# Collecting the first output tile in two free banks during the last attention head

## The chip, the cores and the metric

The kernel runs on one core of a Trainium2 chip. The metric is the device time of one execution in microseconds (us), read as the median of several runs. A profile of one execution on the chip stands beside the times. Its engines are PE (TensorE matmuls; PEld are its weight loads), DVE (VectorE), ACT (ScalarE), POOL (GpSimd) and SP (SyncE, which here only issues transfers). L363 is line 363 of the kernel.

## The reference, cut to what matters

One transformer block on a sequence of 2048 rows of 640 numbers. `h` is a modulated layer norm of `x`; the attention has 32 heads of 128 with keys and values from a cache of 2048 rows; its output goes through `wo`, is scaled by `ga` and added to `x`. A second, mixer-like part follows.

```python
q = (x @ wq) -> (heads, 2048, 128)
p = softmax(q @ k_cache^T * 128 ** -0.5)
o = p @ v_cache                                  # per head
A = o (2048 x 4096) @ wo                         # 4096 = 32 heads x 128
x = x + ga * A
x = x + gb * B(layernorm(x) * (1 + cb) + sb)     # two layer norms, shifts, four products
```

## The kernel before, in words

**Steps.** The sequence is cut into 16 tiles of 128 rows (`NQT`), so there are 32 x 16 = 512 tiles of attention (`NG`), counted by `g`: head `g // 16`, tile `g % 16`. The main loop (L636) runs over steps `s`. In step `s` PE makes the scores of tile `s` in two halves of 1024 columns (`qk`, L342, with the second matmul of each half at L15), into the two halves of the PSUM tensor `Sps`; DVE scales each half, copies it to `negS` and takes its minimum (L675); POOL joins the two minima (L680); ACT writes the exponentials to a slot of `ring` (L683). The score matrix must be transposed before the product with the values. That happens for groups of up to three tiles by a DMA transpose that SP issues (`transpose`, L282 to L286, shown as L284), or for a few single tiles (`PE_AT`) by PE: `t_piece` (L309, transposes at L316) puts a quarter of the tile into one of two banks, `Oaug` or `QPp` (`JB`), and `t_evac` (L320, L323) copies them back to the ring with ACT. Ten steps after its scores (`PVD = 10`) a tile gets its value product (`pv`, L355, matmuls at L363) in `PTp`; ACT copies two tiles at a time out of it (L660), POOL divides by the sum of the exponentials (L540, L547) and writes four tiles to `o_scratch` in DRAM (L554).

**Ring slots.** A planner written in Python (L235 to L277) gives each tile a slot for its exponentials (`PSL`) and one for its transpose (`TSL`). The ring has six windows of three slots (`WIN`) for groups and two single slots (`ONE`) for PE's tiles. `first_of` and `last_of` say in which step a group's window is taken and in which its transpose is issued. By it, in the last head, tiles 497, 504 and 511 go to PE and 498-500, 501-503, 505-507 and 508-510 go by DMA; tile 504's transposes lie in steps 508 and 509, tile 511's in 514 and 515. The exponentials of 508-510 go to slots 0 to 2, which held those of 501-503 until their transpose was done.

**PE's order.** It is the order of the program. In each half step: scores, value product, then at most one piece more: a fifth of a later head's projection (`q_piece`, L296, in all heads but the last) or two transposes. In the last head the two `JB` banks hold only transposes.

**The product with wo.** `load_ot` (L595, shown as L596) fetches a pair of tiles for some heads out of `o_scratch`, transposed, into `OTj`. `a_pe` (L615) multiplies one tile of it with `wo` for some heads (matmuls at L624): for each head one of 512 and one of 128 columns, into a half of `Sps` (`YB`). Tile 0 is made in three parts, `OTC = [0, 12, 24, 32]` heads: two in steps 517 and 518, the last behind the loop; tile 1 has 12 heads in step 520 and the others behind the loop. From then on each tile follows the one before (`a_two`, `a_pe`), with DVE's scaling, sum and norm (`a_s1`, L730, first instruction L732; `a_s2`). The x tiles for the sum come by `load_xt` (L603, L604).

**SP's order** from step 496 on: group 494-496, load of tile pair 0, heads 0 to 11 (step 498), groups 498-500, 501-503, 505-507, load of heads 12 to 23 (step 507), group 508-510, then at step 513 load of heads 24 to 31, x tiles 0 to 3, pair 1 in two halves, and the other x tiles.

Every operation names what it reads and writes (`r=`, `w=`); `Prog` (L20) turns that into semaphore waits.

Of the kernel before, what the change touches and what calls it, by code (L numbers as in the profile page):

```python
# [123 lines left out]
def bass_adaLN_cond__mha_block_cached__mixer_s_mlp__prompt_kernel(  # L124
# [21 lines left out]
    with ExitStack() as es:  # L146
# [9 lines left out]
        if True:  # L156
            with ExitStack() as es1:
# [2 lines left out]
                PVD = 10  # L160
                PE_T = {3: 7, 10: 14, 17: 21, 24: 28, 31: 37}
                PE_AT = {32 * i + t: 32 * i + a for i in range(NG // 32) for t, a in PE_T.items()}
                PE_AT[NG - 1] = NG + 2
                US = KT * (SQ + 4)
                small = sb1("small", [128, 4 * NQT + 32], F32)
                ring = sb1("ring", [128, NS, SK], BF16)
# [74 lines left out]
                def take(opts):  # L241
                    a = min((a for a in opts if free_at[a] is not None), key=lambda a: free_at[a])
                    free_at[a] = None
                    return a
# [10 lines left out]
                    trios.append(m)  # L255
                    todo = todo[len(m):]
                for m in trios:
                    first_of[m[0]] = last_of[m[-1]] = m
                for s in range(NG):
                    end = s >= NG - 10  # L260
                    g = s - PVD
                    if g in PSL and is_pe(g):
                        free_at[TSL[g]] = 100 + s
                    elif g in last_of:
                        free_at[TSL[last_of[g][0]]] = 100 + s + 1
                    if is_pe(s):
                        PSL[s] = TSL[s] = take(ONE)
                    if s in first_of:
                        a = take(WIN[0:3] if end else WIN)
                        for i, g in enumerate(first_of[s]):  # L270
                            PSL[g] = a + i
                    if s in last_of:
                        m = last_of[s]
                        a = take(WIN[3:6] if end else WIN)
                        for i, g in enumerate(m):
                            TSL[g] = a + i
                        free_at[PSL[m[0]]] = 100 + s + 6.5  # L277
# [25 lines left out]
                def q_evac(h, cc):  # L303
# [2 lines left out]
                    G.op("scalar", lambda a: a.copy(QT[:, hb, cc * 512:(cc + 1) * 512], JB[jb]),  # L306
                         r=[("J", jb)], w=[("QT", hb, cc)])

                def t_piece(g, r, q):  # L309
                    jb = bank(("t", g, r))  # L310
                    src = ring[:, PSL[g], :].bitcast(F32)

                    def f(t):
                        for z in range(2 * q, 2 * q + 2):
                            c0 = (4 * r + z) * 128
                            ins = t.transpose(JB[jb][:, z * 128:(z + 1) * 128], src[:, c0:c0 + 128], identf[:])  # L316
                        return ins
                    G.op("tensor", f, r=[("PT", PSL[g], r), "identf"], w=[("J", jb)])

                def t_evac(g, r):  # L320
                    jb = bank(("t", g, r))
                    dst = ring[:, TSL[g], r * 1024:(r + 1) * 1024].bitcast(F32)
                    G.op("scalar", lambda a: a.copy(dst, JB[jb]), r=[("J", jb)], w=[("PT", TSL[g], r)])  # L323

                PIECES = []
                taken = [u for a in PE_AT.values() for u in range(2 * a, 2 * a + 4)]
# [278 lines left out]
                        xt[:, 4 * c0:4 * c1], x2d[c0 * 512:c1 * 512, :].rearrange("(t p) d -> p t d", p=128)),  # L605
                        ("xt", c0), w=[("x1", t) for t in range(4 * c0, 4 * c1)] + ringk(XT0 + 4 * c0 * D, XT0 + 4 * c1 * D))

                OTC = [0, 12 * H // 32, 24 * H // 32, H]
                yn = [0]

                def ybank():
# [3 lines left out]
                def a_pe(j, b=None, parts=(0, 1, 2), hs=None):  # L615
                    if b is None:
                        b = ybank()
                    pr, z = divmod(j, 2)
                    h0, h1 = hs or (OTC[parts[0]], OTC[parts[-1] + 1])

                    def f(t):
                        for c0, cw in NC2:
                            for hh in range(h0, h1):
                                ins = t.matmul(YB[b][:, c0:c0 + cw], OTj[pr % 2][:, 2 * hh + z, :], wo[:, hh, c0:c0 + cw],  # L624
                                               start=(hh == 0), stop=(hh == H - 1))
                        return ins
                    G.op("tensor", f, r=[("OT", pr % 2, i) for i in parts] + [("OTa", pr % 2)] + ["wo", "woz", "wo4"], w=[("S", b)])
                    return b

                def a_two(j):  # L630
                    b = a_pe(j, None, (0,), (0, H // 2))
                    return a_pe(j, b, (1, 2), (H // 2, H))

                YB = [Sps[:, 0:1024], Sps[:, 1024:2048]]
                LAG = 4
                for s in range(NG + PVD + LAG):  # L636
                    h, j = divmod(s, NQT)
                    g_ = s - PVD
                    evacs = []
                    for half in range(2):  # L640
                        if s < NG:
                            qk(s, half)
                        if half == 0 and s in (NG + PVD - 5, NG + PVD - 4):
                            b0 = a_pe(0, None if s == NG + PVD - 5 else b0, (s - NG - PVD + 5,))
                        if half == 0 and s == NG + PVD - 2:
                            b1 = a_pe(1, None, (0,))
                        if 0 <= g_ < NG:
                            pv(g_, half)
                        if h + 1 < H and 2 * s + half in PIECES[h]:
                            cc, q = PIECES[h][2 * s + half]  # L650
                            q_piece(h + 1, cc, q)
                            if q == KT - 1:
                                evacs.append((q_evac, h + 1, cc))
                        for g, r in t_of(s):
                            t_piece(g, r, half)
                            if half == 1:
                                evacs.append((t_evac, g, r))
                    if 0 <= g_ < NG and g_ % 2 == 1:
                        p = g_ // 2
                        G.op("scalar", lambda a, p=p: a.copy(  # L660
                            Of[:, p % 4].rearrange("p z d -> p (z d)")[:, 0:259], PO[:, (p % 2) * 512:(p % 2) * 512 + 259]),
                            r=[("O", p % 2)], w=[("Of", p % 4)])
# [16 lines left out]
                    if s < NG:  # L679
                        G.op("gpsimd", lambda g, r8=r8: g.tensor_scalar(  # L680
                            out=nm[:, r8:r8 + 1], in0=nm0[:, r8:r8 + 1], scalar1=nm1[:, r8:r8 + 1], scalar2=None, op0=ALU.min),
                            r=[("nmh", 0, r8), ("nmh", 1, r8)], w=[("nm", r8)])
                        G.op("scalar", lambda a, s=s, r8=r8: a.activation(  # L683
                            ring[:, PSL[s], :], negS[:, s % 3, :], ACT.Exp, bias=nm[:, r8:r8 + 1], scale=-1.0),
                            r=[("negS", s % 3), ("nm", r8)], w=slot(PSL[s]))
                        for fn, *args in LATE.get(s, ()):
                            fn(*args)
                        if s in last_of:
                            transpose(last_of[s])
                        if j == 2 and h >= 1 and h + 1 < H:  # L690
                            load_k(h + 1)
                        if h + 1 == H and j in (2, PVD + 1):
                            i = 0 if j == 2 else 1
                            load_ot(0, OTC[i], OTC[i + 1], i)
                        if j == (6 if h else 11) and h + 2 < H:
                            load_wq(h + 2)
                        if s == 9 and H > 1:
                            load_k(1)
                        if j == PVD + 1 and h + 1 < H:
                            load_v(h + 1)  # L700
# [5 lines left out]
                    if s == NG + PVD - 9:  # L706
                        G.op("gpsimd", lambda g: g.memset(mhalf, -0.5), w=["mhalf"] + NEG)
                        load_ot(0, OTC[2], OTC[3], 2)
                        load_xt(0, 1)
                        load_ot(1, 0, H // 2, 0)  # L710
                        load_ot(1, H // 2, H, 1)
                    if s == NG + PVD - 7:
                        load_xt(1, NQC)
# [15 lines left out]

                def a_s1(j, b):  # L730
                    u = j % 2
                    G.op("vector", lambda v: v.tensor_mul(out=tmp[:, u], in0=YB[b][:, 0:D], in1=mod_bc[:, 0:D]),  # L732
                         r=[("S", b), "mod"], w=[("tmp", u)] + (TMPK if j < 2 else []))
                    G.op("vector", lambda v: v.tensor_add(out=xt[:, j], in0=tmp[:, u], in1=xt[:, j]),
                         r=[("tmp", u)], w=[("x1", j)])
                    stats_of(0, j, xt[:, j], ("x1", j))
# [80 lines left out]

                for i in range(NQT):
                    if i < NQT - 2:
                        b = a_pe(0, b0, (2,)) if i == 0 else a_pe(1, b1, (1, 2)) if i == 1 else a_two(i) if i in (2, 3, 4, 5) else a_pe(i)  # L820
                    if i == NQT - 3:
                        for z in range(2):
                            G.op("gpsimd", lambda g, z=z: g.memset(us[:, :, z * SQ:z * SQ + 4], 0.0), w=[("usz", z)] + OT0K)  # L823
# [163 lines left out]
```

## Time and profile before

| what | value |
|---|---|
| runs | 1536.43, 1534.05, 1536.42 us; median 1536.42 |
| the profiled execution | 1534.42 us, of which its span is 1532.6 us |
| busy, share of the span | PE 96%, DVE 89%, ACT 82%, POOL 41%; PEld 60% |
| chain that ended last | ACT 71%, PE 20%, DVE 5%, DMA 2% |
| last score product issued (L15) | 1206.95 us |
| last exponential (L683) | starts 1212.80, takes 2.01 us |
| first product with wo (L624) | 1219.95 us |
| third tile's product with wo begins | 1242.01 us |

The span is counted from the first to the last instruction; the rest of the execution's time lies around it. A row of the timeline has the start, the length, the engine, the line, the operation with what it writes and reads, the count of instructions merged, and in brackets the idle time before it with what ended that. SPq is the issuing of transfers by SP: its length is the time that SP was occupied, and the landing comes later. Matmuls overlap, so the distance of two starts says more than a length.

### The profile page before, as it was taken

The numbers are of one execution on the slowest core, as the hardware profiler recorded it, in microseconds if no ns is written. First come the engines' busy times: TensorE is split into PE (matmuls) and PEld (weight loads), VectorE is DVE, ScalarE is ACT, GpSimd is POOL, SyncE is SP. The second block draws the span as 40 slices with busy tenths as digits, with TensorE's granted clock in tenths as the row PEclk, the third lists the DMA queues.
The fourth block names the chain that finished last, engine by engine and source line by source line (L and its number), as shares of the span: only waits on it lengthen the run. The fifth ranks groups of instructions, "written<-read, shape, count | busy, mean of one in ns | idle before, by whom it ended". The sixth has DMA issues, their size and how long they took to land.

```text
span 1532.6 us, 32446 instructions
## 1 busy us (share of the span) xinstructions
PE 1473.7 (96%) x13448; PEld 919.2 (60%) x12664; DVE 1370.6 (89%) x2423; ACT 1256.7 (82%) x1182; POOL 625.5 (41%) x1402
## 2 busy tenths in 40 slices
PE   6899999999999999999999999999999899999999
PEld 3466666666666666666666666666666565554545
DVE  8999999999999999999999999999999546768425
ACT  6999999999999999999999999999999600034230
POOL 1244444444444444444444444444444433333000
PEclk9999999999999999999999999999999999999999
DMA  9999999999999999999999999999999996624101
GB/s 329 251 236 242 235 248 243 243 235 250 226 256 238 241 239 240 241 234 249 227 253 236 239 240 243 235 243 240 247 238 237 236 253 153 139 78 112 35 22 35
DMA packets 1155088, 330.29 MB, mean 216 GB/s; under 512 B 1132986, under 2 KB 1149562, under 8 KB 1154938
## 3 DMA queue, kind: packets, MB, share of 16 engines
q1 hardware_dynamic: 1146448, 307.09, 99.9%
q0 software_dynamic: 6144, 16.79, 3.4%
q10 hardware_dynamic: 2346, 4.34, 0.8%
q8 instruction: 103, 1.69, 0.5%
q14 instruction: 47, 0.39, 0.1%
HBM read 43.48 MB, written 19.40 MB: 41 GB/s over the span
## 4 chain that ended last, share of the span: by engine, by line
ACT 71%; PE 20%; DVE 5%; DMA 2%; issue 2%; SPq 1%; POOL 0%; DVEq 0%; ACTq 0%
ACT ring L683 58%; PE Sps L624 9%; ACT ring L323 5%; DVE negS L675 4%; ACT Of L660 4%; PE Sps L924 4%; ACT kv L306 4%; PE QPp L875 2%; PE Oaug L875 2%; PE Sps L860 1%; DMA kv<-in_A_wq_dram 1%; ACT hTx L465 1%; SPq L221 1%; DMA ring<-ring 1%; PE PTp L363 1%
## 5 line engine op out<-in xcount | busy, mean ns | idle before, releaser
L675 DVE TENSOR_SCALAR_CACHE_REDUCE negS<-Sps 128x1024 f32<-128x1024 f32 x1024 | 1174.1, 1224 | 9.4 <-PE Sps L15 7.0
L683 ACT ACTIVATE ring<-negS,small 128x2048 bf16<-128x2048 f32 x512 | 1133.9, 2479 | 4.4 <-DMA ring<-ring 3.4
L363 PEld LDWEIGHTS PTp<-kv,ring 128*128 128x128 bf16 x8192 | 558.8, 98 | 297.9 <-issue 71.1
L363 PE MATMUL PTp<-kv,ring 128*128 128x129 bf16 x8192 | 646.2, 221 | 9.9 <-DMA ring<-ring 6.0
L15 PE MATMUL Sps<-kv 128*128 128x512 bf16 x1007 | 382.3, 380 | 9.9 <-DVE negS L675 6.5
L680 POOL TENSOR_SCALAR small<-small 128x1 f32<-128x1 f32 x512 | 146.0, 285 | 595.5 <-DVE negS L675 595.4
L349 PE MATMUL Sps<-kv 128*128 128x512 bf16 x957 | 370.0, 387 | 14.8 <-DVE negS L675 1.5
L660 ACT COPY Of<-PTp 128x259 f32<-128x259 f32 x256 | 214.1, 836 | 15.6 <-PE PTp L363 15.6
L547 POOL TENSOR_SCALAR On<-Of,small 128x128 bf16<-128x128 f32 x512 | 189.8, 371 | 13.0
L349 PEld LDWEIGHTS Sps<-kv 128*128 128x128 bf16 x1024 | 98.2, 96 | 134.1 <-DVE negS L675 93.1
L540 POOL TENSOR_TENSOR small<-Of,small 128x4 f32<-128x4 f32 x128 | 133.1, 1040 | 14.0 <-ACT Of L660 14.0
L554 POOL DMA_DIRECT2D o_scratch<-On x128 | 103.8, 811 | 40.7 <-POOL On L547 37.2
L299 PE MATMUL Oaug<-hTx,kv 128*128 128x512 bf16 x254 | 96.5, 382 | 5.3 <-DMA kv<-in_A_wq_dram 3.4
L299 PE MATMUL QPp<-hTx,kv 128*128 128x512 bf16 x263 | 97.9, 379 | 1.1 <-ACT ring L323 0.8
L805 ACT ACT_TABLE_LOAD x1 | 1.3, 1283 | 111.8 <-POOL hTx L823 111.8
L675 DVE DVE_READ_ACCUMULATOR negS<-Sps 128x1 f32 x1024 | 89.9, 88 | 0.0
L323 ACT COPY ring<-Oaug 128x512 f32<-128x512 f32 x80 | 84.0, 1050 | 1.4 <-PE Oaug L316 1.4
L323 ACT COPY ring<-QPp 128x512 f32<-128x512 f32 x80 | 84.5, 1056 | 0.0
L718 POOL TENSOR_SCALAR negS<-negS 128x1 f32<-128x1 f32 x48 | 24.2, 503 | 124.1 <-DVE negS L727 124.1
L732 DVE TENSOR_TENSOR ring<-Sps,mod_bc 128x640 f32<-128x640 f32 x16 | 13.2, 825 | 66.2 <-PE Sps L624 66.2
L624 PE MATMUL Sps<-wo,negS 128*128 128x128 bf16 (+1 forms) x503 | 69.9, 298 | 0.5
L624 PE MATMUL Sps<-wo,hTx 128*128 128x512 bf16 (+1 forms) x502 | 69.3, 297 | 0.5
(99 smaller groups left out, 1065.6 us busy)
## 6 DMA issues: line engine op xcount, KB each, us to landing
kv<-in_A_v_cache_dram SPq DMA_DIRECT2D x32, 512.0 KB, 5.3
o_scratch<-On POOLq DMA_DIRECT2D x128, 128.0 KB, 5.2
kv<-in_A_wq_dram SPq DMA_DIRECT2D x32, 160.0 KB, 3.5
wo<-in_A_wo_dram SPq DMA_DIRECT2D x1, 5120.0 KB, 21.6
ring<-in_A_x_dram SPq DMA_DIRECT2D x5, 640.0 KB, 5.0
ring<-in_w_mod_dram SPq DMA_DIRECT2D x5, 640.0 KB, 8.5
out_dram<-wo SPq DMA_DIRECT2D x15, 160.0 KB, 1.8
ring<-ring SPq DMA_TRANSPOSE x144, 9.5
```

Source lines behind the costliest of these rows:

```text
L15: return t.add_instruction(mybir.InstMatmult(name=t.bass.get_next_instruction_name(), ins=[t.lower_ap(rhs), t.lower_ap(lhsT)], outs=[t.low ...
L299: G.op("tensor", lambda t: t.matmul(JB[jb], wq[:, hb, q, :], hT[:, q, cc * 512:(cc + 1) * 512], start=(q == 0), stop=(q == KT - 1)), r=[(" ...
L323: G.op("scalar", lambda a: a.copy(dst, JB[jb]), r=[("J", jb)], w=[("PT", TSL[g], r)])
L349: ins = (t.matmul if c2 == 0 else partial(same_weights, t))(Sps[:, col:col + 512], QT[:, hb, j * 128:(j + 1) * 128], KTs[:, hb, col:col + ...
L363: ins = t.matmul(ob[:, 0:129], pt, Vaug[:, hb, kt, 0:129], start=(kt == 0), stop=(kt == NKT - 1))
L540: G.op("gpsimd", lambda g: g.tensor_tensor(out=rl[:, 4 * b:4 * b + 4], in0=Of[:].rearrange("p a z d -> p (a z) d")[:, 4 * b:4 * b + 4, 128 ...
L547: G.op("gpsimd", lambda g: g.tensor_scalar(out=On[:, b, z, :], in0=Of[:, 2 * b + z // 2, z % 2, 0:128], scalar1=rl[:, 4 * b + z:4 * b + z ...
L624: ins = t.matmul(YB[b][:, c0:c0 + cw], OTj[pr % 2][:, 2 * hh + z, :], wo[:, hh, c0:c0 + cw], start=(hh == 0), stop=(hh == H - 1))
L660: G.op("scalar", lambda a, p=p: a.copy(Of[:, p % 4].rearrange("p z d -> p (z d)")[:, 0:259], PO[:, (p % 2) * 512:(p % 2) * 512 + 259]), r= ...
L675: G.op("vector", lambda v, half=half, dst=dst, src=src, r8=r8: v.tensor_scalar(out=dst, in0=src, scalar1=-SCALE, scalar2=None, op0=ALU.mul ...
L680: G.op("gpsimd", lambda g, r8=r8: g.tensor_scalar(out=nm[:, r8:r8 + 1], in0=nm0[:, r8:r8 + 1], scalar1=nm1[:, r8:r8 + 1], scalar2=None, op ...
L683: G.op("scalar", lambda a, s=s, r8=r8: a.activation(ring[:, PSL[s], :], negS[:, s % 3, :], ACT.Exp, bias=nm[:, r8:r8 + 1], scale=-1.0), r= ...
```

## The change

In the last head tiles 510 and 511 are now those that PE transposes (steps 513, 514 and 515, 516), and 504 no longer is. The last two DMA groups are 504-506 and 507-509. The last of them takes slots 13 to 15 for its exponentials and 7 to 9 for its transpose, and its transpose is issued one step later than its last tile (step 510). The transposes of 510 and 511 go into banks of the second half of `Sps`, which has no scores any more, so that the two `JB` banks stay free.

These two banks collect tile 0's product with `wo` (`y0`): one head in each half step of steps 506 to 511, behind the value product, twelve in all. Eight heads of tile 1 (`y1`, in the first half of `Sps`) follow the second half of step 512's value product; four more of tile 1 and heads 12 to 30 of tile 0 follow step 516's. Head 31 of tile 0 and heads 12 to 31 of tile 1 come behind the loop. `OTC` becomes `[0, 12, 31, 32]`, so the second load has 19 heads and the third one. The loads' steps become 496 and 506; in SP's queue the first still comes after group 494-496, and the second after group 504-506. The load of pair 1's first half moves ahead of x tiles 0 to 3. DVE's first scaling of tile 0 reads two banks with two instructions.

```diff
-                PE_AT[NG - 1] = NG + 2
+                PE_AT[NG - 2], PE_AT[NG - 1] = NG + 1, NG + 3
+                del PE_AT[NG - 8]
...
-                    first_of[m[0]] = last_of[m[-1]] = m
+                    first_of[m[0]] = last_of[m[-1] + (m is trios[-1])] = m
...
-                        a = take(WIN[0:3] if end else WIN)
+                        a = take([13] if m is trios[-1] else WIN[0:3] if end else WIN)
...
-                        a = take(WIN[3:6] if end else WIN)
+                        a = take([7] if m is trios[-1] else WIN[3:6] if end else WIN)
...
+                def t_bank(g, r):
+                    if g >= NG - 2:
+                        return Sps[:, (2 + r) * 512:(3 + r) * 512], [("S", 1), ("Sb", 2 + r)]
+                    jb = bank(("t", g, r))
+                    return JB[jb], [("J", jb)]
...
-                OTC = [0, 12 * H // 32, 24 * H // 32, H]
+                OTC = [0, 12 * H // 32, H - 1, H]
...
+                def y0(h0, h1):
+                    def f(t):
+                        for jb, (c0, cw) in enumerate(NC2):
+                            for hh in range(h0, h1):
+                                ins = t.matmul(JB[jb][:, 0:cw], OTj[0][:, 2 * hh, :], wo[:, hh, c0:c0 + cw],
+                                               start=(hh == 0), stop=(hh == H - 1))
+                        return ins
+                    G.op("tensor", f, r=[("OT", 0, i) for i in range(3) if OTC[i] < h1 and h0 < OTC[i + 1]] + [("OTa", 0), "wo", "woz", "wo4"],
+                         w=[("J", 0), ("J", 1)])
+
+                def y1(h0, h1):
+                    a_pe(1, 0, [i for i in range(3) if OTC[i] < h1 and h0 < OTC[i + 1]], (h0, h1))
...
+                Y0S = NG - 6
+                TAIL = {(s, z): [(y0, 2 * (s - Y0S) + z, 2 * (s - Y0S) + z + 1)] for s in range(Y0S, NG) for z in range(2)}
+                TAIL[(NG, 1)] = [(y1, 0, 8)]
+                TAIL[(NG + 4, 1)] = [(y1, 8, OTC[1]), (y0, OTC[1], OTC[2])]
...
-                        if half == 0 and s in (NG + PVD - 5, NG + PVD - 4):
-                            b0 = a_pe(0, None if s == NG + PVD - 5 else b0, (s - NG - PVD + 5,))
-                        if half == 0 and s == NG + PVD - 2:
-                            b1 = a_pe(1, None, (0,))
...
+                        for fn, *args in TAIL.get((s, half), ()):
+                            fn(*args)
...
-                        if h + 1 == H and j in (2, PVD + 1):
-                            i = 0 if j == 2 else 1
+                        if h + 1 == H and j in (0, NQT - 6):
+                            i = int(j > 0)
                             load_ot(0, OTC[i], OTC[i + 1], i)
...
                         load_ot(0, OTC[2], OTC[3], 2)
+                        load_ot(1, 0, H // 2, 0)
                         load_xt(0, 1)
-                        load_ot(1, 0, H // 2, 0)
                         load_ot(1, H // 2, H, 1)
...
-                        b = a_pe(0, b0, (2,)) if i == 0 else a_pe(1, b1, (1, 2)) if i == 1 else a_two(i) if i in (2, 3, 4, 5) else a_pe(i)
+                        b = (y0(OTC[2], H) or 0) if i == 0 else a_pe(1, 0, (1, 2)) if i == 1 else a_two(i) if i in (2, 3, 4, 5) else a_pe(i)
```

More of the change, by code (lines that the diff above doesn't have):

```diff
@@ L268, in bass_adaLN_cond__mha_block_cached__mixer_s_mlp__prompt_kernel @@
                     if s in first_of:
-                        a = take(WIN[0:3] if end else WIN)
-                        for i, g in enumerate(first_of[s]):
+                        m = first_of[s]
+                        a = take([13] if m is trios[-1] else WIN[0:3] if end else WIN)
+                        for i, g in enumerate(m):
                             PSL[g] = a + i
@@ L307, in q_evac @@
                          r=[("J", jb)], w=[("QT", hb, cc)])
+                def t_bank(g, r):
[3 more added lines that the diff above has]
+                    return JB[jb], [("J", jb)]
                 def t_piece(g, r, q):
-                    jb = bank(("t", g, r))
+                    dst, keys = t_bank(g, r)
                     src = ring[:, PSL[g], :].bitcast(F32)
@@ L315, in f @@
                             c0 = (4 * r + z) * 128
-                            ins = t.transpose(JB[jb][:, z * 128:(z + 1) * 128], src[:, c0:c0 + 128], identf[:])
+                            ins = t.transpose(dst[:, z * 128:(z + 1) * 128], src[:, c0:c0 + 128], identf[:])
                         return ins
-                    G.op("tensor", f, r=[("PT", PSL[g], r), "identf"], w=[("J", jb)])
+                    G.op("tensor", f, r=[("PT", PSL[g], r), "identf"], w=keys)
                 def t_evac(g, r):
-                    jb = bank(("t", g, r))
+                    src, keys = t_bank(g, r)
                     dst = ring[:, TSL[g], r * 1024:(r + 1) * 1024].bitcast(F32)
-                    G.op("scalar", lambda a: a.copy(dst, JB[jb]), r=[("J", jb)], w=[("PT", TSL[g], r)])
+                    G.op("scalar", lambda a: a.copy(dst, src), r=keys[-1:], w=[("PT", TSL[g], r)])
                 PIECES = []
@@ L626, in f @@
                         return ins
-                    G.op("tensor", f, r=[("OT", pr % 2, i) for i in parts] + [("OTa", pr % 2)] + ["wo", "woz", "wo4"], w=[("S", b)])
-                    return b
+                    G.op("tensor", f, r=[("OT", pr % 2, i) for i in parts] + [("OTa", pr % 2)] + ["wo", "woz", "wo4"],
+                         w=[("S", b)] + ([("Sb", 2), ("Sb", 3)] if b == 1 else []))
+                    return b
+                def y0(h0, h1):
[9 more added lines that the diff above has]
+                    a_pe(1, 0, [i for i in range(3) if OTC[i] < h1 and h0 < OTC[i + 1]], (h0, h1))
                 def a_two(j):
@@ L731, in a_s1 @@
                     u = j % 2
-                    G.op("vector", lambda v: v.tensor_mul(out=tmp[:, u], in0=YB[b][:, 0:D], in1=mod_bc[:, 0:D]),
-                         r=[("S", b), "mod"], w=[("tmp", u)] + (TMPK if j < 2 else []))
+                    for c0, c1, src, key in [(0, D, YB[b], ("S", b))] if j else [(0, 512, JB[0], ("J", 0)), (512, D, JB[1], ("J", 1))]:
+                        G.op("vector", lambda v, c0=c0, c1=c1, src=src: v.tensor_mul(out=tmp[:, u, c0:c1], in0=src[:, 0:c1 - c0], in1=mod_bc[:, c0:c1]),
+                             r=[key, "mod"], w=[("tmp", u)] + (TMPK if j < 2 else []))
                     G.op("vector", lambda v: v.tensor_add(out=xt[:, j], in0=tmp[:, u], in1=xt[:, j]),
```

## The prediction

> **What bounds the kernel now.** I read the chain of waits first. It runs through the attention loop on ACT's exponentials (L683), leaves them at 1214.8 us and is from 1219.95 us to the end almost only TensorE (L624, then L924; one DMA of 7.6 us at 1380). So behind the loop PE is the bound, and any microsecond by which its unbroken run of products starts earlier is a microsecond of the total. I then read PE's timeline where the loop ends (start, length, engine, line, operation, count, idle time and releaser):
>
> ```profile
> 1206.95 0.38 PE L15 MATMUL Sps<-kv 128*128 128x512 bf16 x1
> 1207.16 0.63 PE L363 MATMUL PTp<-kv,ring 128*128 128x129 bf16 x8
> 1208.42 2.05 PE L363 MATMUL PTp<-kv,ring 128*128 128x129 bf16 x32 [0.63 <-ACT Of L660]
> 1212.96 0.64 PE L363 MATMUL PTp<-kv,ring 128*128 128x129 bf16 x8 [2.50 <-ACT Of L660]
> 1214.86 0.44 PE L316 MATMUL Oaug<-identf,ring 128*128 128x128 f32 x2 [1.25 <-ACT ring L683]
> ...
> 1223.93 3.42 PE L624 MATMUL Sps<-wo,hTx 128*128 128x512 bf16 x23
> 1227.18 2.04 PE L363 MATMUL PTp<-kv,ring 128*128 128x129 bf16 x32
> 1229.06 3.42 PE L624 MATMUL Sps<-wo,hTx 128*128 128x512 bf16 x23
> ...
> 1242.01 17.33 PE L624 MATMUL Sps<-wo,negS 128*128 128x512 bf16 x126
> ```
>
> The last score product is issued at 1206.95; its value product is out by 1207.16 + 8 x 0.0585 = 1207.63. The third tile's product with wo starts at 1242.01, and from there PE has no gap that matters (16.94 of 17 us busy up to 1259). Between the two lie 34.4 us. The work in them: 160 value products (tiles 502 to 511) at 0.0585 (1.87 us for 32) = 9.4; two tiles x 32 heads x 0.2716 (24 matmuls, 12 heads, take 3.26 us from 1229.06 to the next row) = 17.4; 8 transposes, 1.0. Sum 27.8. The other 6.6 us are waits of about 0.8, 2.5 and 1.4 us, and a slow clock. The table by stage (window, busy time of PE, PEld, DVE, ACT, POOL, granted clock, DMA) shows that:
>
> ```profile
> 1207.00:1213.00 6.00, 2.88 (x43) 2.41 (x42) 2.38 (x4) 6.00 (x7) 3.47 (x8) 1.00 1.29 230
> 1213.00:1216.00 3.00, 1.75 (x19) 1.56 (x20) 0.00 (x0) 2.07 (x2) 1.08 (x3) 0.89 1.11 186
> 1216.00:1219.00 3.00, 3.00 (x27) 2.85 (x26) 0.00 (x0) 0.94 (x3) 2.40 (x6) 0.54 1.24 295
> ```
>
> What makes PE wait is ACT, late since one exponential waited for a transfer to leave its ring slot; and the transfers stand one behind another in SP's queue (second and third fence):
>
> ```profile
> 1206.10 2.00 ACT L683 ACTIVATE ring<-negS,small 128x2048 bf16<-128x2048 f32 x1 [3.40 <-DMA ring<-ring]
> ```
> ```profile
> 1184.63 5.55 SPq L596 DMA_TRANSPOSE hTx<-o_scratch  x1
> 1190.28 20.05 SPq L284 DMA_TRANSPOSE ring<-ring  x3
> 1210.38 4.39 SPq L596 DMA_TRANSPOSE hTx<-o_scratch  x1
> 1214.82 6.15 SPq L284 DMA_TRANSPOSE ring<-ring  x1
> 1221.07 2.35 SPq L596 DMA_TRANSPOSE hTx<-o_scratch  x1
> 1224.01 0.37 SPq L604 DMA_DIRECT2D ring<-in_A_x_dram  x1
> 1224.43 11.48 SPq L596 DMA_TRANSPOSE negS<-o_scratch  x2
> ```
>
> SP issues without a pause from 1184.63 to 1210: a group of three tiles takes about 6.2 to 7.4 us, and lands 7.7 to 9.8 us after its issue starts. This queue decides what is late next.
>
> **The change part by part.**
>
> (1) Twelve heads of the first tile go into steps 506 to 511, one piece (a 512 and a 128 column matmul, 0.27 us) per half step. A half step is set by DVE: its reductions start every 1.145 us. PE fills 0.91 of that (two score products 0.44, eight value products 0.47); a gap of 0.23 remains, in which the transposes of 501 and 504 now lie without changing the pace. A piece exceeds it by 0.04: twelve pieces make PE 0.5 us late at the loop's end, and the scores are ready 0.4 us before DVE takes them, so DVE loses at most 0.1. 3.26 us leave the path behind the loop, 0.67 come back (lag and last piece). The first piece needs load part 0. It is behind the same group in SP's queue as before, so issues at 1184.63 and lands 8.2 later, at 1192.8; the piece's place is 1195.0. Cover 2.2 us.
>
> (2) Tile 504 goes back to the DMA and 510 to PE: 504-506 and 507-509 are the last groups. Four fewer transposes in the loop, 8 more behind it: +1.0 us.
>
> (3) The last group's exponentials write slots 13 to 15, free since value product 496, instead of 0 to 2. The 3.40 us wait of ACT goes: exponential 508 can start at its minimum's time, 1202.5, the last ends at about 1211.4 instead of 1214.8. PE's waits of 2.5 and 1.4 us on ACT go with it. Nothing is gained on DVE's 1.56 us stall itself, since PE had its scores already.
>
> (4) Order in SP's queue: group 504-506 takes the place of 505-507 (1203.91, lands 9.7 later, 1213.7); then load part 1 at 1210.38, now 19 heads instead of 12; then the last group; then a load of one head (was 8); then the second pair's first half, the x tiles and the second half. A 19 head load isn't in the trace. Rows by head: 12 heads 4.39 and 5.55 (0.37, 0.46), 16 heads 6.19 (0.39), 32 heads 7.8 (0.245). So 4.7 to 8.8 us; I take 0.366, the row at this very place of the queue: 6.95. The last group issues at 1217.3 (1215.1 to 1219.2) and lands 9.2 later, as the one at 1214.82 does: **1226.5** (1224.3 to 1228.4). Load part 1 itself lands 1213.7 + 19/12 x 3.9 = 1219.9 (12 heads landed 3.9 behind the group before).
>
> (5) PE behind the loop, in the new order. Step 511 ends at 1208.3. Value product 502 0.94, eight heads of tile 1 (2.17): 1211.4. These fill the old waits. 503 with four transposes 1.45: 1212.9. 504 waits for 1213.7. 504, 505, 506 with twelve transposes 4.35: 1218.0; four heads 1.09: 1219.1; 19 heads of tile 0 wait for 1219.9 and take 5.16: 1225.1. 507 waits for the last group, 1226.4: PE idles 1.3 us. Then 507 to 511 4.7, head 31 0.27, 20 heads of tile 1 5.43: **1236.8**, against 1242.0. **Saved: 5.2 us.** The three new waits (0.8, 0.8, 1.3) lie 5 us or more apart.
>
> (6) Edits at nothing: DVE reads tile 0 from two banks (one more instruction, some 0.2 us more than the 0.82 of one) while PE has 5.4 us of tile 1 before it. The x tiles land at about 1235 to 1237 instead of 1228.3, so tile 0's add waits 2 to 4 us; DVE idles 2.5 us in each 8.69 us tile and catches up in two, and the banks aren't reused before 1245. The second pair's halves land at about 1234 and 1238, needed at 1236.8 and 1241.1; the thinnest cover is those 2.8 us. All later transfers follow PE's own progress, so the rest moves along whole.
>
> **A rule weighed.** The clock row of 0.54 stands behind idle stretches of 2.5 and 1.4 us with only 0.5 us of work between them; in the window of the 0.8 us gap it stayed at 1.00, and in the loop's windows with transposes too (1200 to 1207). The Trainium skill (TensorE: Matmul & The Clock Gate, "HAM oscillation") says that PE falls to half clock after an idle window of some 3.4 us. The trace agrees, with 0.54 after 3.9 us of nearly unbroken idling. Its Part 4 (PE-mode transpose) says that transposes don't count as busy work in the same way; by that, the 16 transposes between short value products in steps 513 to 516 speak against this change. The loop's 1.00 speaks against the rule here. If the clock did fall there, the old loss (6.6 less 4.7 to 4.9 of idle, 1.7 us) would come back ahead of the wait for the last group, which hides 1.3 of it: 0.4 us less saved, 1531.6.
>
> **The sum.** The profiled execution took 1534.42 (span 1532.6 and 1.8 around it): 1529.2 after. The runs shown lie at 1534.05, 1536.42 and 1536.43, the median 2.0 above the profiled one; I forecast from the median: 1536.42 - 5.2 = **1531.2**.
>
> **Rivals.**
> - The 19 head load is quick (32 head row: 4.7 us). Then the last group lands at 1224.3, PE's own work decides (1225.1), saving 6.5: 1529.9. For it: the DMA carries less once the loop ends. Up to 8.2 (1528.2) if the other two waits vanish too. Chance 0.15.
> - It is slow (0.46 a head, as the load inside the loop): the last group lands at 1228.4, saving 3.2: 1533.2. For it: the rows by head spread that widely; against it: the row at the same place says 0.37. Chance 0.15; with the scatter of the runs half of it falls within 0.2%.
> - The clock falls at the wait for the last group itself and stays down over a stage as in 1216 to 1219: 1.7 us, saving 3.5: 1532.9. Against it: the new wait is half the old ones. Chance 0.05.
> - Slower: the last group stands behind a longer load. If that load blocks SP for over 6.95 + 5.2 = 12.2 us (0.64 a head), value product 507 is so late that the old order was better; at 14 us it is 1.8 us slower: 1538.3. Against it: no row by head is over 0.46, and the heads that it now adds were written to scratch by 1183. Chance 0.07.
> - The change doesn't do what it says: pieces stall the loop (load part 0 later than 1195.0) or don't fit, and PE's lag takes what the missing wait gives. 1 us of lag costs nothing (the 1.3 us wait hides it), so it takes 3 us or more to lose over half; saving 2: 1534.4. Chance 0.06.
>
> The forecast holds 0.52, from 1529.9 to 1532.4. With the other cases, scatter of 1 to 2 us between runs included, the range is 1527.8 to 1534.0. Beyond 0.2% (3.1 us, about what a measurement of this kernel can tell from no change) faster: all of the forecast but its edge, the first rival, half of the second, the clock's: 0.74. Same 0.18, slower 0.08.
>
> **What would show it.** ACT has no wait for ring<-ring at step 508 and its last exponential ends near 1211.4. DVE runs at 1.145 us through step 511. PE shows L624's successor for tile 0 in the loop, no wait on Of, a wait of about 1.3 us on the last group near 1225, no granted clock under 0.9, and tile 2 begins near 1236.8. The 19 head load takes 6 to 8 us of SP. It is wrong if PE waits over 3 us for the last group, if the clock falls, or if tile 2's loads are late.

## The result, and the profile after

The changed kernel took 1550.24 us (median of 6, 1547.28 to 1553.49) against 1536.41 of the kernel before (6 runs, 1534.05 to 1538.97). The ratio of the two is 1.0091, with a 95% interval of 1.0079 to 1.0103: slower by 14 us, where 5 faster had been forecast. Every ratio below is to the kernel before as it ran beside that kernel. The profiled execution took 1549.14, its span is 1547.3.

PE's timeline of the changed kernel, as the first fence of the prediction showed it for before (value products are L371 now, the product with wo L643 for tile 0 and L632 for the other tiles):

```profile
1209.48 0.38 PE L15 MATMUL Sps<-kv 128*128 128x512 bf16 x1
...
1215.28 0.64 PE L371 MATMUL PTp<-kv,ring 128*128 128x129 bf16 x8 [0.19 <-DMA ring<-ring]
...
1221.80 4.28 PE L643 MATMUL Oaug<-wo,hTx 128*128 128x512 bf16 x19 [1.11 <-DMA hTx<-o_scratch]
...
1228.68 2.98 PE L371 MATMUL PTp<-kv,ring 128*128 128x129 bf16 x48 [1.55 <-DMA ring<-ring]
1247.07 3.54 PE L371 MATMUL PTp<-kv,ring 128*128 128x129 bf16 x32 [15.40 <-DMA ring<-in_A_x_dram]
...
1256.15 6.02 PE L632 MATMUL Sps<-wo,negS 128*128 128x512 bf16 x38
```

The loop ends 2.5 us later than in the other trace (1209.48 against 1206.95), so I read stretches from the last score product on: to the third tile's product 35.06 us before, 46.67 now. The three waits that were forecast are there (0.2, 1.1 and 1.55). A fourth isn't in the forecast: 15.40 us ahead of the value products of tiles 510 and 511 (x32), and what ends it is a load of x, which no value product should need. ACT isn't late any more, and no wait stands ahead of its last exponential:

```profile
1211.61 2.00 ACT L707 ACTIVATE ring<-negS,small 128x2048 bf16<-128x2048 f32 x1
```

SP's queue shows the load of x as its last row:

```profile
1211.50 7.45 SPq L604 DMA_TRANSPOSE hTx<-o_scratch  x1
1219.04 6.05 SPq L286 DMA_TRANSPOSE ring<-ring  x1
1225.18 1.20 SPq L604 DMA_TRANSPOSE hTx<-o_scratch  x1
1226.44 5.32 SPq L604 DMA_TRANSPOSE negS<-o_scratch  x1
1231.81 0.57 SPq L612 DMA_DIRECT2D ring<-in_A_x_dram  x1
1232.42 6.25 SPq L604 DMA_TRANSPOSE negS<-o_scratch  x1
1238.78 0.53 SPq L612 DMA_DIRECT2D ring<-in_A_x_dram  x1
```

It is issued at 1238.78 and lands 8.2 us later, at 1247.0: the moment at which PE goes on. The table by stage (columns as in the prediction) adds a slow clock behind the wait:

```profile
1213.00:1220.00 7.00, 6.76 (x92) 6.14 (x91) 0.00 (x0) 3.28 (x7) 4.08 (x8) 1.00 1.15 174
...
1226.00:1232.00 6.00, 4.12 (x68) 3.77 (x66) 0.00 (x0) 0.67 (x2) 1.60 (x3) 1.00 0.77 164
1232.00:1247.00 15.00, 0.00 (x0) 0.00 (x0) 0.00 (x0) 0.08 (x1) 1.62 (x4) 0.66 1.08 275
1247.00:1250.00 3.00, 2.93 (x28) 2.94 (x29) 0.00 (x0) 0.00 (x0) 0.00 (x0) 0.50 0.00 0
```

**The code names the reason.** The x tiles lie in the ring from element 3072 on, 640 a tile (L559, L565 of the kernel before); a slot has 2048. Tiles 4 to 15 take elements 5632 to 13311, that is slots 2 to 6, and their load is in step 515 of the program. Slot 6 is one of the two for single tiles. Before, it held tile 504, whose value product is in step 514, one step ahead of the load. The change gives it to tile 510, whose value product is in step 520. The load is then the last writer of the slot, and the value product has to wait for it, at the end of SP's queue. By this order half of tile 510's slot holds x, and not its exponentials, when the value product reads it: by the code, the conflict costs the tile its result as well as the kernel its time. The same holds below for tile 510 in number 3, for tile 511 in numbers 1 and 4 and for tile 504 in number 11; the other kernels don't have the conflict.

### The profile page after: what moved, and what is told of

It reads as the page before. It is cut to its first block, busy times and chain, and to the rows that moved or that the text cites. A ratio compares the mean times of both kernels' runs of the same rounds, so it can differ in the third digit from the quotient of the medians.

```text
span 1547.3 us, 32447 instructions
## 1 busy us (share of the span) xinstructions
PE 1472.8 (95%) x13449; PEld 918.2 (59%) x12664; DVE 1370.5 (89%) x2424; ACT 1257.1 (81%) x1182; POOL 626.4 (40%) x1402
## 4 chain that ended last, share of the span: by engine, by line
ACT 66%; PE 19%; DVE 8%; issue 3%; DMA 3%; POOL 1%; SPq 1%; POOLq 0%; DVEq 0%
ACT ring L707 54%; PE Sps L632 8%; DVE negS L699 7%; ACT ring L331 4%; ACT Of L684 4%; PE Sps L949 4%; ACT kv L308 4%; PE QPp L900 2%; PE Oaug L900 2%; DMA ring<-in_A_x_dram 1%; PE Sps L885 1%; DMA ring<-ring 1%; DMA kv<-Of 1%; SPq L604 0%; PE Oaug L822 0%
## 5 line engine op out<-in xcount | busy, mean ns | idle before, releaser
L707 ACT ACTIVATE ring<-negS,small 128x2048 bf16<-128x2048 f32 x512 | 1115.5, 2391 | 2.9 <-POOL small L704 2.7
L371 PEld LDWEIGHTS PTp<-kv,ring 128*128 128x128 bf16 x8192 | 559.1, 98 | 317.9 <-issue 82.0
L371 PE MATMUL PTp<-kv,ring 128*128 128x129 bf16 x8192 | 647.0, 221 | 24.9 <-DMA ring<-in_A_x_dram 15.4
L684 ACT COPY Of<-PTp 128x259 f32<-128x259 f32 x256 | 191.3, 747 | 31.5 <-PE PTp L371 31.5
L331 ACT COPY ring<-QPp 128x512 f32<-128x512 f32 x78 | 76.2, 977 | 0.0
L331 ACT COPY ring<-Oaug 128x512 f32<-128x512 f32 x78 | 75.7, 971 | 0.0
L632 PE MATMUL Sps<-wo,negS 128*128 128x128 bf16 (+1 forms) x503 | 70.1, 298 | 0.5
L953 DVE TENSOR_TENSOR ring<-Sps,ring 128x640 f32<-128x640 f32 x15 | 12.4, 824 | 59.5 <-PE Sps L949 59.5
L308 ACT CAST kv<-QPp 128x512 bf16<-128x512 f32 x65 | 62.2, 956 | 1.3 <-PE QPp L301 1.3
```

The lines of the kernel that those rows point to most:

```text
L331: G.op("scalar", lambda a: a.copy(dst, src), r=keys[-1:], w=[("PT", TSL[g], r)])
L371: ins = t.matmul(ob[:, 0:129], pt, Vaug[:, hb, kt, 0:129], start=(kt == 0), stop=(kt == NKT - 1))
L684: G.op("scalar", lambda a, p=p: a.copy(Of[:, p % 4].rearrange("p z d -> p (z d)")[:, 0:259], PO[:, (p % 2) * 512:(p % 2) * 512 + 259]), r= ...
L707: G.op("scalar", lambda a, s=s, r8=r8: a.activation(ring[:, PSL[s], :], negS[:, s % 3, :], ACT.Exp, bias=nm[:, r8:r8 + 1], scale=-1.0), r= ...
```

## The experiments

Theory A: this shared slot is the whole loss, and without it the forecast holds. Theory B: the wait shown is only the last of several, and the longer load or PE's lag decide. The kernel before ran beside each group, with medians of 1536.15 (first four), 1536.53 (next four), 1536.91 (fills) and 1536.09 us (last).

**1. Another slot for tile 510.**

```diff
-                        PSL[s] = TSL[s] = take(ONE)
+                        PSL[s] = TSL[s] = take([0] if s == NG - 2 else ONE)
```

> The changed kernel with one slot moved: tile 510's exponentials and their transpose go to ring slot 0 instead of slot 6. Slot 6 is one of those that the load of x tiles 4 to 15 overwrites (slots 2 to 6), slot 0 isn't. In the changed kernel PE waits 15.4 us for that load ahead of tile 510's value product, and the clock is at 0.50 behind it. Theory A (the shared slot is the whole loss): the wait goes, tile 510 follows 509 at once, the third tile begins 1231.5 + 1.87 + 0.27 + 5.43 = 1239.1 instead of 1256.2, so 17 us less than the changed kernel (about 1533, by the forecast's own sum 1531). Theory B (the wait shown is only the last of several, the longer load and PE's lag decide): the time stays above 1543, as PE waits elsewhere. With the slot shared, the changed kernel reads x in one half of tile 510's slot; this one doesn't.

Measured: 1558.47 us, ratio 1.0137 (1.0122 to 1.0152), 8 more than the changed kernel. Neither theory's number, since the edit did something else: the planner gave the freed slot 6 to tile 511. PE's timeline shows the wait one place further ahead, at the last transposes of 511 (step 516), where the 19 heads stand behind it too:

```profile
1245.17 0.69 PE L324 MATMUL Sps<-identf,ring 128*128 128x128 f32 x2 [27.39 <-DMA ring<-in_A_x_dram]
```

The wait moved with the slot. (Here tile 511's slot is the one half full of x.) The run doesn't decide between A and B.

**2. The slot kept, the last x tiles loaded later.**

```diff
-                        load_xt(1, NQC)
+                        load_xt(1, NQC - 1)
+                    if s == NG + PVD - 2:
+                        load_xt(NQC - 1, NQC)
```

> The changed kernel, slot 6 kept for tile 510, but the load of x tiles 12 to 15, which alone reaches into slot 6, is issued behind tile 510's value product (step 520) instead of in step 515. Theory A: same as with slot 0, about 1533, no wait of PE for the x load; x tiles 12 to 15 are needed only some 100 us later. Theory B: above 1543. A third theory C (it isn't the slot's sharing but the load's traffic at this time that holds PE up, the load being 1920 KB): only a quarter of the load moves, so three quarters of the wait stay, 1546.

Measured: 1532.26 us, ratio 0.9982 (0.9965 to 1.0), 18 less than the changed kernel. Two of its ten runs lie near 1540, so its gain over the kernel before isn't clear of the noise; the 18 us are. It is A's number. Theory C, by which the traffic of the load holds PE up, wanted 1546 and falls; B wanted over 1543. PE waits only for the last group:

```profile
1225.91 4.86 PE L371 MATMUL PTp<-kv,ring 128*128 128x129 bf16 x80 [1.21 <-DMA ring<-ring]
...
1236.31 17.55 PE L632 MATMUL Sps<-wo,negS 128*128 128x512 bf16 x128
```

**3. The slot shared, the x load further ahead in SP's queue.**

```diff
                         load_xt(0, 1)
-                        load_ot(1, H // 2, H, 1)
                     if s == NG + PVD - 7:
                         load_xt(1, NQC)
+                        load_ot(1, H // 2, H, 1)
```

> The changed kernel with the slot still shared (so one half of tile 510's slot still holds x when its value product reads it), but in SP's queue the load of x tiles 4 to 15 now stands ahead of the second half of tile pair 1 instead of behind it; that half took SP 6.25 us. Theory A: the wait ends 6.3 us earlier, so 6 us less than the changed kernel, about 1544; the wait is about 9 us. Theory B: no change, 1550, since the sum of the loads is the same. If the clock is what costs most: less than 6, since the wait stays over 3.4 us.

Measured: 1546.89 us, ratio 1.0065 (1.0042 to 1.0087): 3.4 less than the changed kernel, not 6, and a wait of 11.77 us instead of 9. The direction is A's, and SP's waits show where the other 3 us stayed (the line waited for, us in total, times, longest us):

```profile
SPq L612 <- DMA ring<-in_A_x_dram: 3.6, 1, 3.6
```

The second x load waits for the first, since both write slot 2. Counted from the last score product, the x load landed 34.3 us behind it (1241.9 less 1207.57) instead of 37.5: 3.2 earlier, and the time is 3.4 less. The four runs scatter from 1544.3 to 1550.4 and the interval overlaps that of the changed kernel, so the 3.4 are weak evidence; the 3.2 of the trace are the better sign. The clock takes the same in both (3.65 and 3.54 us for the 32 value products), so it doesn't tell the two kernels apart.

**4. No pieces in the loop, on the first kernel of this list.**

```diff
-                TAIL = {(s, z): [(y0, 2 * (s - Y0S) + z, 2 * (s - Y0S) + z + 1)] for s in range(Y0S, NG) for z in range(2)}
-                TAIL[(NG, 1)] = [(y1, 0, 8)]
+                TAIL = {}
+                TAIL[(NG, 1)] = [(y0, 0, OTC[1]), (y1, 0, 8)]
```

> The kernel with slot 0 for tile 510, and the twelve pieces of tile 0 taken out of steps 506 to 511 and put in one stretch behind the value product of step 512. 3.26 us of PE's work come back behind the loop, 0.7 of lag goes. Theory A with the forecast's part 5 (the last group's transfer sets the end): PE's new waits of 0.2, 1.1 and 1.5 us in the changed kernel absorb it, so within 0.7 us of the kernel with slot 0. If PE's own work sets the end: 2.6 to 3.3 us more than the kernel with slot 0.

Measured: 1557.87 us, 0.6 less than the kernel it was built on, which is within their scatter. That kernel's wait of 27.39 us is here too, with 25.77. It shows only that such a wait swallows 3.26 us of PE's work. It was repeated as number 6.

**5. Slots 0 and 19 for tiles 510 and 511.**

```diff
-                        PSL[s] = TSL[s] = take(ONE)
+                        PSL[s] = TSL[s] = take([0] if s == NG - 2 else [19] if s == NG - 1 else ONE)
```

> The changed kernel with both single tiles kept off the x tiles' slots: tile 510 in slot 0 and tile 511 in slot 19 (in the first attempt the planner had given the freed slot 6 to tile 511, and the wait of 27.4 us came ahead of its last transposes). No load is moved. Theory A (a shared slot is the whole loss): no wait for the x load, the same time as the kernel whose last x tiles are loaded late, 1532, within 1.5 us; third tile 27.6 us behind the last score product, as there, against 35.1 in the kernel before and 46.8 in the changed one. Theory B (the late x load itself gave that kernel its time, by taking traffic out of the crowded stretch): 1536 or more.

Measured: 1531.83 us, ratio 0.9969 (0.9958 to 0.998). The forecast for the change was 1531.2. Its timeline, and SP's issue of the last group:

```profile
1209.63 0.38 PE L15 MATMUL Sps<-kv 128*128 128x512 bf16 x1
...
1221.24 4.27 PE L643 MATMUL Oaug<-wo,hTx 128*128 128x512 bf16 x19 [0.35 <-DMA hTx<-o_scratch]
...
1228.45 4.86 PE L371 MATMUL PTp<-kv,ring 128*128 128x129 bf16 x80 [1.87 <-DMA ring<-ring]
...
1238.85 17.55 PE L632 MATMUL Sps<-wo,negS 128*128 128x512 bf16 x126
```
```profile
1218.52 6.55 SPq L286 DMA_TRANSPOSE ring<-ring  x1
```

29.2 us from the last score product to the third tile (27.6 had been expected, as in number 2's trace), 5.8 less than before and 17.5 less than in the changed kernel: the wait of 15.4, 1.7 of half clock in the 32 value products (3.54 against 1.87), and 0.4 in the three other waits (2.85 in sum against 2.45). No load was moved in the program, and the time is that of number 2, so theory B has nothing left.

**6 to 8. What the parts are worth, on number 5.** Number 6 takes the pieces out of the loop by the edit of number 4; number 7 cuts the 19 head load to 12; number 8 also puts the last group ahead of that load, and twelve heads each of tiles 0 and 1 behind the last value product. The first change below is in 7 and 8, the second in 8 alone; 8's lines that move the heads are left out.

```diff
-                OTC = [0, 12 * H // 32, H - 1, H]
+                OTC = [0, 12 * H // 32, 24 * H // 32, H]
...
-                        if h + 1 == H and j in (0, NQT - 6):
+                        if h + 1 == H and j in (0, NQT - 1):
```

> The kernel with slots 0 and 19, and the twelve pieces taken out of steps 506 to 511 and put in one stretch behind the value product of step 512. 3.26 us of PE's work come back behind the loop, 0.7 of lag goes. If the last group's transfer sets the end, as the forecast had it: PE's waits (1.2 to 1.5 us for the last group, up to 1.1 for the 19 heads) absorb most of it, at most 1 us over the kernel with slots 0 and 19. If PE's own work sets it: 2.6 to 3.3 us over it.

> The kernel with slots 0 and 19, and the second load cut from 19 heads to 12, as in the kernel before (the third has 8 again; seven heads of tile 0 go behind the last value product). SP's 6.4 to 7.4 us for it become some 4.4, so the last group's transfer lands 2 to 3 us earlier, while PE reaches it 1.9 us earlier. If that transfer sets the end: the wait of 1.2 us goes, 1 us less than the kernel with slots 0 and 19, 1531. If PE's own work sets it: the same time.

> As the one before, and the last group's transpose goes ahead of the 12 head load in SP's queue; twelve heads of tiles 0 and 1 each move behind value product 511. The group lands near 1219, when PE has just reached tile 507, so no wait for it is left; the load has 4.7 us more of value products ahead of it. Expected: the same as the one before within 0.5 us, or 0.5 less if that still waits. If a wait for the load appears: up to 1 us more.

Measured: 1533.0 (ratio 0.9979, 0.997 to 0.9988), 1532.45 (0.9972, 0.996 to 0.9984) and 1534.77 (0.9987, 0.9978 to 0.9995). Number 6 lies 1.2 over number 5 by the medians, nearer to "the transfer sets the end" (1 at most) than to PE's own 2.6 to 3.3, though the intervals overlap. The traces say the same more strongly: PE waits for the last group in both, 1.75 us in number 6 and 1.87 in number 5. The group was issued at the same time (1218.50 and 1218.52) and took 11.0 us to land in number 6 against 9.9. So the 1.1 us between the two traces at the third tile (1239.99 and 1238.85) lie in that transfer and not in PE's extra work, and what the pieces are worth isn't shown; the medians give about 1.2 us. Numbers 7 and 8 gained nothing, and the traces say why. In 7 PE came earlier than the group and waited longer (first row); the clock fell, and 80 value products took 6.43 us instead of 4.86. In 8 PE still waited 1.44 for the last group, and the second half of tile pair 1 was late (second row):

```profile
1225.41 6.43 PE L371 MATMUL PTp<-kv,ring 128*128 128x129 bf16 x80 [2.26 <-DMA ring<-ring]
```
```profile
1242.84 12.99 PE L632 MATMUL Sps<-wo,negS 128*128 128x512 bf16 x94 [1.52 <-DMA negS<-o_scratch]
```

**9 and 10. Work into the wait for the last group.** Heads of tile 1 move ahead of value product 507. The first line with a plus is number 9, built on number 7, the second is number 10, built on number 5; the line behind the loop that gives up these heads is left out.

```diff
-                TAIL[(NG + 4, 1)] = [(y1, 8, OTC[1]), (y0, OTC[1], OTC[2])]
+                TAIL[(NG + 4, 1)] = [(y1, 8, OTC[1]), (y0, OTC[1], OTC[2]), (y1, OTC[1], OTC[2])]
...
+                TAIL[(NG + 4, 1)] = [(y1, 8, OTC[1]), (y0, OTC[1], OTC[2]), (y1, OTC[1], 20)]
```

> The kernel with slots 0 and 19 and the 12 head load, and twelve heads of tile 1 (12 to 23, loaded with tile 0's) moved from behind value product 511 to ahead of 507. There PE waited 2.26 us for the last group and then ran some 3 us at half clock (80 value products in 6.43 us instead of 4.86). 3.26 us of work now fill the wait. If the wait for the last group is what is left: both go, 3.8 us less than without the fill, third tile 27.1 us behind the last score product, 1529 to 1530. Rival: the second half of tile pair 1 is next (needed 4.35 us behind the start of the third tile, lands at about the same time), it takes back up to 1.5 us: 1530 to 1531. If the wait isn't PE's bound: 1532.4 as before.

> The kernel with slots 0 and 19 and the 19 head load, and eight heads of tile 1 (12 to 19) moved from behind value product 511 to ahead of 507: 2.17 us of work fill the 1.87 us wait for the last group. If that wait is what is left: 1.9 us less than the kernel with slots 0 and 19, 1530. Rival: the second half of tile pair 1 is late by up to 1 us and takes part of it back: 1531. If the wait isn't PE's bound: 1531.8.

Measured: 1531.99 (ratio 0.9971, 0.9958 to 0.9984) and 1532.88 (0.9976, 0.9965 to 0.9988), both with runs that scattered more (1528.0 to 1537.4). Number 10's profiled execution is its quickest (1527.96) and shows what was meant, no wait of PE and 26.25 us from the last score product to the third tile; in number 9's the rival came, a wait of 2.42 for the second half of pair 1. By the medians neither beats number 5, so the fills are not shown to help.

**11. The mechanism without the change.** The kernel before, with one line moved.

```diff
                         load_ot(1, H // 2, H, 1)
-                    if s == NG + PVD - 7:
                         load_xt(1, NQC)
```

> The kernel before, none of the change in it, with one line moved: the load of x tiles 4 to 15 stands two steps earlier (513 instead of 515), at the same place in SP's queue. In this kernel slot 6 holds tile 504, whose value product is in step 514: now one step behind the load in the program instead of one step ahead of it, so half of that slot holds x when it is read. If a slot shared across the program's order is enough to make the loss: PE waits ahead of value product 504 until the x load lands, 1245.6 in the trace of before (issue 1236.02, 9.6 to landing), 32.6 us behind the 1212.96 at which it ran, and some 2 us go to half clock: 1566 to 1572. If the loss needs other parts of the change (the pieces, the longer load): 1536 to 1540.

Measured: 1565.0 us, ratio 1.0179 (1.0159 to 1.02). PE's timeline:

```profile
1210.11 2.50 PE L363 MATMUL PTp<-kv,ring 128*128 128x129 bf16 x40
1246.40 1.05 PE L363 MATMUL PTp<-kv,ring 128*128 128x129 bf16 x8 [33.79 <-DMA ring<-in_A_x_dram]
```

A wait of 33.8 us, 32.6 expected, from a slot and the place of one line alone. The time is 29 over before and not 30 to 36: the two later waits of that kernel on ACT, 2.5 and 1.4 us, are gone behind it.

## Why the prediction was wrong, step by step

- **Step 2 failed, and with it step 6, which costs the late x tiles at nothing.** Step 2 moved tile 510 to PE and counted its transposes, not the slot that it takes. Step 6 followed x tiles 0 to 3 to the additions that read them, and not the x tiles to the slots that they overwrite; the load of tiles 4 to 15 is only in its last sentence, that all later transfers follow PE's own progress. Here PE had to follow that transfer. The plan of slots and the x tiles' place were both in the code; the check that was missing is: who still reads what this transfer writes, and is that ahead of it in the program? It costs 15.4 us of wait and 1.7 of half clock, and 18.4 in the time (1550.24 less 1531.83). Numbers 2 and 5 take the conflict away in two ways and the loss goes; number 11 brings it into the kernel before and a loss of 29 us comes.
- **The last rival had the right form** ("doesn't do what it says") with the wrong place: it looked at load part 0 and at PE's lag. The slower rival, a blocked SP behind the long load, didn't come: 6.0 to 7.45 us for 19 heads, 6.95 forecast, 12.2 needed.
- **Step 1 holds.** The pieces run in the loop; with them the scores come every 1.17 us, 12 x 0.025 = 0.3 late in sum (0.5 was forecast), and DVE keeps 1.145. What the step doesn't say is that the 3.3 us less 0.7 which the pieces take off the path are worth little: the three waits of step 5 (0.8, 0.8 and 1.3) are more than these 2.6 and would have hidden them. Number 6 is in line with that: about 1.2 in the medians, and in the trace not even this from PE's work. The transposes that this step calls those of 501 are tile 497's, in steps 501 and 502.
- **Step 3 holds.** ACT has no wait for a ring slot, and its last exponential ends 4.1 us behind the issue of the last score product (1211.61 + 2.00 less 1209.48), against 7.9 before (1212.80 + 2.01 less 1206.95).
- **Steps 4 and 5 hold in size.** Number 5 shows the last group issued at 1218.52 and landed at 1228.4. Its last score product is 2.7 us later than in the trace of before, so that is 1215.8 and 1225.7 in the forecast's times, which had 1217.3 and 1226.5. PE's waits are 0.2, 0.35 and 1.87 against 0.8, 0.8 and 1.3. Saved are 5.8 us in the stretch against 5.2, and 4.7 in the medians. That the sum comes so near is in part luck: each of the three waits misses by 0.5 to 0.6, and they cancel in part. Step 4's rows by head also leave out the load of 8 heads in its own fence (2.35 us, 0.29 a head); 19 heads took 0.32 to 0.39 a head. No run shows by itself how much of the 4.7 comes from step 3.
- **The rule weighed.** The transposes of steps 513 to 516 ran at a clock of 1.00 in the changed kernel: the Trainium skill's remark on them (TensorE: Matmul & The Clock Gate, Part 4) didn't show, in a stretch where they stand between value products. Its other rule ("HAM oscillation") is met again by 0.50 behind the wait of 15.4.

## What to carry to other kernels

When tiles change their place in a planned buffer, list for each slot who writes and who reads it after the move, in program order, and every later transfer that reuses the bytes; a wait that the program's bookkeeping of reads and writes (`Prog`) adds on its own is named in the trace by a tensor that the waiting instruction has no use for. An experiment on a planned buffer must fix all the slots, or the conflict moves with the one that came free. Behind a removed wait the next in the same queue sets the end: here 3.3 us of PE's work were worth about 1.2 in the medians, and the traces don't show that it was they.

## What the runs showed of the hardware

Short waits can halve PE's clock. Number 3 waited 2.02 us for a group of transposes; stages of a microsecond from its table:

```profile
1214.00:1215.00 1.00, 0.00 (x0) 0.00 (x0) 0.00 (x0) 0.00 (x0) 0.90 (x3) 1.00 0.04 10
1215.00:1216.00 1.00, 0.80 (x10) 0.75 (x11) 0.00 (x0) 0.00 (x0) 1.00 (x3) 0.89 1.24 280
1216.00:1217.00 1.00, 1.00 (x11) 0.98 (x9) 0.00 (x0) 0.00 (x0) 0.70 (x2) 0.50 1.28 290
```

The clock was full while PE idled and fell to 0.50 only after it had gone on, for 3.4 us (0.22, 3 and 0.20, worked out from the means of 0.89 and 0.90). In number 7 it fell 0.9 us after a wait of 2.26, and in number 9 near the end of a wait of 2.42, for 3.4 us both times. Waits of 1.55, 1.75 and 1.87 us (the changed kernel, numbers 6 and 5) left it at 1.00 just behind them. The Trainium skill (TensorE: Matmul & The Clock Gate, "HAM oscillation") gives some 3.4 us of idling; here 2.0 was enough once. Number 3's wait also has PE's transposes on both sides, which those of numbers 7 and 9 have not. Whether the length of the wait, its place in time or the work around it decides isn't settled by so few waits.
